# An attention and GLU kernel on one core: a planner's order replaced by an order written down as a string

## The chip, the cores and the metric

The kernel runs on one core of one Trainium2 chip. The metric is device time in microseconds, from one launch. The number of a kernel is the median of its runs; a profile is one further execution, with its own time.

## The reference

All arrays are float32, and all products must keep about that precision. The input x has 2048 tokens of 512 features.

```python
xn = layernorm(x)                                    # 2048 x 512
q, k, v = split(xn @ wqkv)                           # 32 heads of 16
p = softmax(q @ k.T * 16 ** -0.5)                    # per head, 2048 x 2048, no mask
s = (p @ v) @ wo                                     # heads joined
h = (xn @ w_gate) * (xn @ w_up)                      # 2048 x 1792
g = silu(h @ w_down)
out = x + s * g
```

## The kernel before

**Units and turns.** The 32 heads form eight groups of four, and the tokens four blocks of 512 queries. One group with one block is a unit; there are 32 units (`NU`). A unit takes 16 turns, one for each 128 keys. A turn needs, for each of the four heads, a transposed score (`expo`, called t): one matmul of 50 rows into a PSUM bank, and one exponential on ScalarE into an SBUF tile `e`. Then `pv` multiplies the four tiles with the values, for four heads side by side in the array's columns, and adds into one PSUM bank of its own. The trace shows a turn of `pv` as eight matmuls, and two turns in a row as sixteen.

**The maxima.** The exponentials need each query's row maximum, which is an extra operand row of the t matmul. So every score is also computed the other way round (`score`, called s), one matmul of 48 rows into a bank and one `tensor_reduce` on VectorE (the tile `mx`). When a unit has its 64 scores of this kind, `maxima` reduces them further on VectorE, with a small subtraction on GpSimd (`mm`), and `rest` transposes them (`mt`), stores them to DRAM (`MD`) and loads them into the rows of the query tile (`qs`). Only then may the unit's first t run. Scores run `LEAD` = 21 turns ahead of exponentials.

**Products.** Everything else on TensorE is a list of 202 outs, each a product of 128 x 512: projections of q and k (26), the GLU's gate and up products (112), its down products (48, in three thirds per token block), and the last projection (16). Float32 operands are split into a high and a low part on GpSimd, ScalarE and VectorE, and three terms are summed. An out uses the array by halves: all its terms for the lower 64 rows (code `f`), then, after a tiny read of the bank by ScalarE (`look`), all for the upper 64 rows (`F`). Scores t and s also use one half each, the lower (t, s) or the upper (T, S), by the head. Two matmuls on different halves run side by side, so TensorE's time is counted in slots of one lower and one upper matmul.

**Evacuation.** A finished projection or gate product, and the first third of a down product, is copied by ScalarE; an up product is multiplied with the gate by VectorE, then split (`hidden`); further thirds are added by VectorE. After a unit's last turn `heads` transposes the sums (VectorE), divides by the sum (`rc`, `on`), transposes back and stores (`OD`).

**Banks.** PSUM holds eight banks: one for `pv`, seven (`POOL`) for scores and outs.

**Order.** TensorE, ScalarE and VectorE run in the order in which the program issues their instructions; that of the other engines and of the DMA queue is left to the framework. The stretch `early` (layer norm, first projections, values, the first 84 scores) is laid out by hand and is not touched. Behind it, the class `Order` plans while the program is built: it keeps an estimated clock for each of the three engines, and in each `step` chooses what runs next, from constants at the head of the file (`SLOT`, `TURN`, `EXP_STEP`, `MAX_STEP` and the like). A slot with t on one half and s on the other goes first, then t or s with a product on the other half, then products; a `turn` of one or two batches of `pv` when their exponentials are thought to be done. It takes the bank that has been free longest. Evacuations and looks are queued as tasks with due times and run when the engine is thought idle. The last projection of the last token block lacks the last four heads (`kept`, `final`): these are added at the end by twelve more matmuls, when `last_heads` has split them; the loop at the end of `body` calls `final` for two tiles at a time as soon as they are ready.

```python
            if ops is None:
                ops = {x: "f" for x in (0, 1) if can[x]}
                if len(ops) < 2 and ready:
                    return self.turn(ks)
                if not ops:
                    return self.wake()
```

Of the kernel before, what the change touches and what calls it, by code (L numbers as in the profile page):

```python
# [19 lines left out]
P = 128  # L20
# [15 lines left out]
PACE, PACE0 = 4.95, 0  # L36
MOST = 4
HELD, T_APART, S_APART, APART = 2, 3, 6, .4
NEARLY, LEAN, AHEAD = 1, .1, 16
SLOT, ENTER, TURN, LEAVE, AGAIN = .229, .105, .857, .10, .105  # L40
T_SEEN, EXP_STEP, EXP_FREE, E_READY = .43, .494, .66, .65
S_SEEN, MAX_STEP, MAX_FREE = .46, .609, .75
COPY, HIDDEN, PRODUCT, LOOK, LOOK_SEEN, RECIP = .60, .63, .68, .16, .15, .30
MAXIMA, MAXIMA_WAIT, REST, KNOWN = .45, 4.0, .15, 6.0
RELEASE, IDLE, LATE, SPLIT_WAIT, SILU_GAP = .15, .1, 3.0, 12.0, 12.0
ACT_AHEAD, DVE_AHEAD, ACT_FULL, DVE_FULL = .5, .9, .75, 1.2
# [7 lines left out]
def body(ctx, tc, x, wqkv, wo, wg, wu, wd, out):  # L54
# [209 lines left out]
    class Out:  # L264

        def __init__(self, name, sums, evac, begin=None, ready=None, need=None, more=(), kept=False):
            self.name, self.sums, self.evac, self.begin = name, sums, evac, begin
            self.ready, self.need, self.more, self.kept = ready, need, more, kept
            self.looked = None
            self.over = False  # L270

        def open(self, k, o):
            self.bank, self.o = k, o
            if self.begin:
                self.begin()
            sums = self.sums()
            self.terms = [*(self.more() if self.more else ()), *sums], sums
            self.at = [0, 0]

        def blocked(self, x):  # L280
            return self.need is not None and not self.need(self.at[x], x)

        def product(self, x):
            n, ts = self.at[x], self.terms[x]
            rows = (LOWER, UPPER)[x]
            l, r = ts[n]
            last = n == len(ts) - 1
            nc.tensor.matmul(self.o, l[rows], r[rows], start=x == 0 and n == 0,  # L288
                             stop=last and (x == 0 or not self.kept), skip_group_check=x == 1)
            self.at[x] += 1  # L290
            return last

    class Order:

        def __init__(self, outs):
            self.pe = self.act = self.dve = 0.0
            self.free = [0.0] * POOL
            self.outs, self.next = outs, None
            self.low = self.high = None
            self.mid = []  # L300
            self.held = 0
            self.done = [0, 0]
            self.tpos, self.spos = [0, 0], [2 * LEAD, 2 * LEAD]
            self.tout, self.sout = [], []
            self.es, self.eready = {}, {}
            self.turns = self.begun = 0
            self.after = False
            self.tasks = {"act": [], "dve": []}
            self.number = 0
            self.known = {0: -100.0}  # L310
            self.fetch()

        def fetch(self):
            self.next = next(self.outs, None)

        def task(self, engine, ready, cost, fn, gate=None, urgent=False, then=None):
            self.number += 1
            self.tasks[engine].append((ready, self.number, cost, fn, gate, urgent, then))
            self.tasks[engine].sort(key=lambda t: t[:2])

        def run_tasks(self):
            again = True
            while again:
                again = False
                for engine in ("act", "dve"):
                    for n, (ready, _, cost, fn, gate, urgent, then) in enumerate(self.tasks[engine]):
                        if ready > self.pe:
                            break
                        idle = getattr(self, engine) <= self.pe + IDLE
                        if (idle or urgent or self.pe - ready > LATE) and (gate is None or gate()):  # L330
                            del self.tasks[engine][n]
                            begin = max(getattr(self, engine), ready)
                            setattr(self, engine, begin + cost)
                            fn()
                            if then:
                                then(begin + cost)
                            again = True
                            break

        def bank(self):  # L340
            k = min((t, k) for k, t in enumerate(self.free) if t is not None and t <= self.pe)[1]
            return k, pool(k)

        def banks(self):
            return sum(t is not None and t <= self.pe for t in self.free)

        def may_open(self):
            return (self.low is None and self.next is not None
                    and (self.held < HELD or self.held == HELD and self.nearly())
                    and (self.next.ready is None or self.next.ready()))  # L350

        def nearly(self):
            o = self.high
            return not self.mid[1:] and (o is None or len(o.terms[1]) - o.at[1] <= NEARLY)

        def lean(self, x):
            return LEAN * (AHEAD - (self.done[0] - self.done[1])) * (1 if x == 0 else -1)

        def can_low(self):
            if self.low is None:  # L360
                return self.may_open() and self.banks() > 0
            return not self.low.blocked(0)

        def can_high(self):
            if self.high is None:
                return bool(self.mid) and self.mid[0].looked is not None and self.mid[0].looked <= self.pe
            return not self.high.blocked(1)

        def do_low(self):
            if self.low is None:  # L370
                o, self.low = self.next, self.next
                k, bank = self.bank()
                self.free[k] = None
                self.held += not o.kept
                o.open(k, bank)
                self.fetch()
            o = self.low
            self.done[0] += 1
            if o.product(0):
                self.low = None  # L380
                self.mid.append(o)

                def done(t, o=o):
                    o.looked = t + LOOK_SEEN
                self.task("act", self.pe + T_SEEN, LOOK, lambda: nc.scalar.activation(look, o.o[0:1, 0:1], AF.Copy),  # L385
                          urgent=True, then=done)

        def do_high(self):
# [3 lines left out]
            self.done[1] += 1  # L392
            if o.product(1):
                self.high = None
                o.over = True
                if not o.kept:
                    def gone(t, o=o):
                        self.free[o.bank] = t + RELEASE
                        self.held -= 1
                    o.evac(self.pe + T_SEEN, gone)  # L400

        def do_t(self, x, late):
# [5 lines left out]
            k, o = self.bank()  # L408
            self.tpos[x] += 1
            i, kt = divmod(n, 16)  # L410
            e = expo(i, kt, j, o)
            begin = max(self.act, self.pe + T_SEEN + late)
            self.act = begin + EXP_STEP
            self.free[k] = begin + EXP_FREE
            self.tout.append(self.free[k])
            self.es.setdefault(n, {})[j] = e
            self.eready[n] = begin + E_READY

        def do_s(self, x, late):
            p = self.spos[x]  # L420
            r, j = p // 2, 2 * (p % 2) + x
            k, o = self.bank()
            self.spos[x] += 1
            si, sr = divmod(r, 16)
            score(si, sr, j, o)
            begin = max(self.dve, self.pe + S_SEEN + late)
            self.dve = begin + MAX_STEP
            self.free[k] = begin + MAX_FREE
            self.sout.append(self.free[k])
            if min(self.spos) == 32 * (si + 1) and max(self.spos) >= 32 * (si + 1) and sr == 15:  # L430
                self.task("dve", self.dve, MAXIMA, lambda: maxima(si), urgent=True,
                          then=lambda t: self.task("dve", t + MAXIMA_WAIT, REST, lambda: rest(si),
                                                   then=lambda t: self.known.__setitem__(si, t + KNOWN)))

        def turn(self, ks):
            for n in ks:
                pv(n // 16, n % 16, self.es.pop(n))
                del self.eready[n]
            self.turns += len(ks)
            self.pe += ENTER + TURN * len(ks) + LEAVE  # L440
            self.after = True
            if self.turns % 16 == 0:
                heads(self, self.turns // 16 - 1)

        def t_allowed(self, x):
            n = self.tpos[x] // 2
# [720 lines left out]
```

## Time and profile before

| | before |
|---|---|
| median of 3 runs | 1828.31 us (1823.27 to 1832.83) |
| profiled execution: time, span | 1832.05 us, 1830.3 us |
| TensorE busy | 1797.4 us, 13,568 matmuls |
| VectorE busy | 1433.9 us |
| ScalarE busy | 1238.7 us |
| GpSimd busy | 588.8 us |
| mean granted TensorE clock | 0.988 of full speed |
| first t matmul | 115.25 us after the span's start |
| start of the last batch of `pv` | 1808.37 us |

The span is that of the instructions on the core; the time also holds what lies around it. In the profile PE is TensorE, PEld its weight loads, DVE VectorE, ACT ScalarE, POOL GpSimd, SP the engine that issues the DMAs. A line of a group reads: line of the program, engine, operation, output<-inputs by the program's names, shapes, count | busy us, mean ns of one | idle time of its engine before them and what ended it. A line of the timeline has start us, length us and the group; `x8` is the number of instructions merged into it. In the chain of work that ended last a line has start us, length us and what held the end. A row of waits has the total in us, how often, and the longest. A row of stretches has the stretch, its length, the busy time of PE, PEld, DVE, ACT and POOL (instructions in brackets), the granted clock, and share and rate of the DMA engines.

### The profile page before, as it was taken

Reading aid. Unit: us, or ns where it says so; the run is one execution under the profiler, and the core shown is the slowest. Engines: PE = TensorE matmul, PEld = TensorE weight load, DVE = VectorE, ACT = ScalarE, POOL = GpSimd, SP = SyncE. Lnnn points to the kernel's source line nnn. Section 1 sums busy time; section 2 is a strip of 40 time slices with the busy share of each in tenths; the row PEclk is TensorE's granted clock in tenths of the full one; section 3 lists DMA queues with packets and bytes.
Section 4 is the critical chain, followed back from the end, with each engine's and each line's share of the span. In section 5 each row is a group of like instructions: output and inputs, shape, how many; then the busy total and the mean of one; then the engine's idle time right before and its main releaser. Section 6 shows DMA issues by size and latency. Waiting matters only on the chain.

```text
span 1830.3 us, 34996 instructions
## 1 busy us (share of the span) xinstructions
PE 1797.4 (98%) x13568; PEld 1057.7 (58%) x13568; DVE 1433.9 (78%) x2433; ACT 1238.7 (68%) x2487; POOL 588.8 (32%) x649
## 2 busy tenths in 40 slices
PE   8899999999999999999999999999999999999998
PEld 6566655565655565555555555656555665554555
DVE  7487877888878888878888788888887888878832
ACT  5147777776766767667676767767676777767674
POOL 5312333530523244143042523314163241332230
PEclk9899999999999999999999999999999999999999
DMA  5425532610231222321024211321234120112232
GB/s 196 112 67 188 200 127 103 159 52 22 73 74 50 77 67 68 62 64 51 22 81 108 80 39 57 70 43 53 73 91 91 33 68 25 56 39 85 71 121 70
DMA packets 117234, 145.79 MB, mean 80 GB/s; under 512 B 12620, under 2 KB 74060, under 8 KB 114380
## 3 DMA queue, kind: packets, MB, share of 16 engines
q1 hardware_dynamic: 117068, 143.55, 27.3%
q8 instruction: 107, 1.75, 0.4%
q14 instruction: 59, 0.48, 0.1%
HBM read 95.94 MB, written 47.45 MB: 78 GB/s over the span
## 4 chain that ended last, share of the span: by engine, by line
PE 92%; DMA 3%; DVE 2%; POOL 1%; ACT 1%; issue 0%; SPq 0%; ACTq 0%; POOLq 0%; DVEq 0%
PE b L288 32%; PE pv L980 26%; PE b L969 16%; PE b L941 15%; PE v L211 2%; DVE mx L943 1%; DMA qs<-MD 1%; PE p L211 1%; PE s L941 1%; DMA MD<-mt 0%; DMA ks<-KD 0%; ACT e L971 0%; DMA wdr<-in_wd_dram 0%; DMA qs<-QD 0%; DMA ks<-in_x_dram 0%
## 5 line engine op out<-in xcount | busy, mean ns | idle before, releaser
L943 DVE TENSOR_REDUCE mx<-b 128x1 f32<-128x512 f32 x1964 | 1232.8, 683 | 287.7 <-PE b L941 136.9
L971 ACT ACTIVATE e<-b 128x512 f32<-128x512 f32 x2048 | 1109.4, 600 | 475.4 <-PE b L969 242.2
L969 PE MATMUL b<-qs,ks 50*128 50x512 f32 x2048 | 776.3, 418 | 7.6 <-DMA qs<-MD 6.0
L941 PE MATMUL b<-ks,qs 48*128 48x512 f32 x1964 | 758.5, 424 | 0.7 <-DVE mx L943 0.3
L980 PE MATMUL pv<-e,V 128*32 128x512 f32 x4096 | 515.2, 605 | 0.2 <-DVE tr L1007 0.2
L969 PEld LDWEIGHTS b<-qs,ks 50*128 50x128 f32 x2048 | 366.4, 186 | 173.0 <-DVE mx L943 47.3
L941 PEld LDWEIGHTS b<-ks,qs 48*128 48x128 f32 x1964 | 338.8, 186 | 197.2 <-ACT e L971 66.4
L980 PEld LDWEIGHTS pv<-e,V 128*32 128x32 f32 x4096 | 98.8, 109 | 218.0 <-issue 207.7
L288 PE MATMUL b<-fh,w1h 64*128 64x512 f32 x504 | 201.0, 402 | 0.6 <-ACT look L385 0.3
L288 PE MATMUL b<-fh,w0h 64*128 64x512 f32 x500 | 199.1, 400 | 0.0
L288 PE MATMUL b<-fh,w1l 64*128 64x512 f32 x504 | 198.4, 398 | 0.0
L288 PE MATMUL b<-fl,w1h 64*128 64x512 f32 x504 | 197.8, 396 | 0.0
L288 PE MATMUL b<-fh,w0l 64*128 64x512 f32 x500 | 196.7, 397 | 0.0
L288 PE MATMUL b<-fl,w0h 64*128 64x512 f32 x500 | 196.6, 395 | 0.0
L288 PE MATMUL b<-dh,hh 64*128 64x512 f32 x448 | 162.7, 403 | 0.7 <-ACT hh L253 0.5
L288 PE MATMUL b<-dh,hl 64*128 64x512 f32 x448 | 158.9, 400 | 2.3 <-POOL hl L254 2.1
L288 PE MATMUL b<-dl,hh 64*128 64x512 f32 x448 | 158.6, 400 | 0.0
L288 PEld LDWEIGHTS b<-fh,w0h 64*128 64x128 f32 x500 | 92.8, 186 | 16.0 <-issue 5.7
L288 PEld LDWEIGHTS b<-fh,w1h 64*128 64x128 f32 x504 | 93.1, 186 | 15.5 <-issue 4.4
L288 PEld LDWEIGHTS b<-fh,w1l 64*128 64x128 f32 x504 | 93.2, 186 | 12.5 <-issue 6.7
L288 PEld LDWEIGHTS b<-fh,w0l 64*128 64x128 f32 x500 | 92.9, 186 | 9.2 <-issue 3.4
L288 PEld LDWEIGHTS b<-fl,w0h 64*128 64x128 f32 x500 | 92.9, 186 | 9.0 <-issue 2.9
(165 smaller groups left out, 1905.8 us busy)
## 6 DMA issues: line engine op xcount, KB each, us to landing
w1r<-in_wg_dram SPq DMA_DIRECT2D x56, 256.0 KB
w0r<-in_wu_dram SPq DMA_DIRECT2D x56, 256.0 KB
wdr<-in_wd_dram SPq DMA_DIRECT2D x56, 256.0 KB
qs<-QD SPq DMA_DIRECT2D x64, 192.0 KB
ks<-KD SPq DMA_DIRECT2D x12, 768.0 KB
KD<-hl SPq DMA_DIRECT2D x16, 512.0 KB
QD<-hl SPq DMA_DIRECT2D x16, 512.0 KB
OD<-tr SPq DMA_DIRECT2D x31, 256.0 KB
```

The lines of the kernel that those rows point to most:

```text
L211: nc.tensor.matmul(o, l(d), r(d), start=k == d == 0, stop=k == 2 and d == ND - 1)
L288: nc.tensor.matmul(self.o, l[rows], r[rows], start=x == 0 and n == 0, stop=last and (x == 0 or not self.kept), skip_group_check=x == 1)
L941: nc.tensor.matmul(o, QS[i][b:b + KB, pr, t * P:(t + 1) * P], k[b:b + KB, pr, kc * 512:(kc + 1) * 512], start=True, stop=True)
L943: nc.vector.tensor_reduce(MX[i][:, j, t, kc:kc + 1], o, axis=AX.X, op=OP.max)
L969: nc.tensor.matmul(o, k[b:b + KR, pr, kt * P:(kt + 1) * P], QS[i][b:b + KR, pr], start=True, stop=True)
L971: nc.scalar.activation(e, o, AF.Exp, scale=DH ** -0.5)
L980: nc.tensor.matmul(fst["pv"][32 * j:32 * j + 32], V[:, kt, h0:h0 + 32], es[j], start=kt == 0, stop=kt == NT - 1)
```

## The change

The planner goes. In its place stands a string, `ORDER`, of some 14,200 characters that a search over orders has found, and a class that reads it. Each letter issues one thing: t, T, s, S a score on the lower or upper half, with a digit for its PSUM bank; o (with a bank) the first lower matmul of the next out, f a further one, F an upper one; v and w one or two turns of `pv`; l a look; e and d an evacuation on ScalarE or VectorE; h the split of a hidden tile; y a quarter of the silu; m and r `maxima` and `rest`; x, c, b the three steps of `heads`; Q the load and split of one token block's heads for the last projection.

```diff
-PACE, PACE0 = 4.95, 0
...
-SLOT, ENTER, TURN, LEAVE, AGAIN = .229, .105, .857, .10, .105
...
+ORDER = """
+o0T1ffT2fS3fT4fT1ffS5fS6ffs3S2fS4o1ls5fS6fFfFfFfFfFfFfFfFfFfFs3Fls2Fs4S5eo6FfFfFt3Ft0FfFt2FfFs4Fs3Ft5S0fFfFfS2efT4fS5f
...
+fFfFfFfFfFfFo3FlfFfdfFfFfFfFfFfFfFfFfFvlxFFFcFbFFFFF
+"""
...
+        def t(self, x, k):
             p = self.tpos[x]
             n, j = p // 2, 2 * (p % 2) + x
             if n == self.begun:
                 self.begun += 1
                 round_begins(n)
             self.tpos[x] += 1
+            self.es.setdefault(n, {})[j] = expo(*divmod(n, 16), j, pool(k))
...
+            if min(self.spos) == 32 * (i + 1):
+                def whole():
+                    maxima(i)
+                    self.then("r", lambda: rest(i))
+                self.then("m", whole)
...
+        def run(self, order):
+            codes = iter(order)
+            for code in codes:
+                if code in "ts":
+                    getattr(self, code)(0, int(next(codes)))
+                elif code in "TS":
+                    getattr(self, code.lower())(1, int(next(codes)))
+                elif code == "o":
+                    self.low_product(int(next(codes)))
+                elif code == "f":
+                    self.low_product()
+                elif code == "F":
+                    self.high_product()
+                elif code in "vw":
+                    for _ in range("_vw".index(code)):
+                        self.v()
+                elif code == "Q":
+                    prepare(int(next(codes)))
+                else:
+                    self.todo[code].pop(0)()
...
         order_ = Order(outs(wq0))
-        todo = list(range(4))
-        while not order_.over():
-            order_.step()
...
+        order_.run(ORDER.replace("\n", ""))
+        last_heads()
+        for t in range(4):
             final(t)
```

The functions that evacuate an out (`evac` and its tasks with due times) become plain functions that the letters e, d, h and y call, and `ending_outs` loses its conditions of readiness. `last_heads` and all four `final` now stand behind the whole string.

656 lines of the change are left out of this document (273 added, 383 removed).

## Prediction

> **What bounds the kernel now.** I read the page first: busy time by engine, the shares of the chain that ended last, and the costliest groups.
>
> ```profile
> span 1830.3 us, 34996 instructions
> ...
> PE 1797.4 (98%) x13568; PEld 1057.7 (58%) x13568; DVE 1433.9 (78%) x2433; ACT 1238.7 (68%) x2487; POOL 588.8 (32%) x649
> ...
> PE 92%; DMA 3%; DVE 2%; POOL 1%; ACT 1%; issue 0%; SPq 0%; ACTq 0%; POOLq 0%; DVEq 0%
> ...
> L943 DVE TENSOR_REDUCE mx<-b 128x1 f32<-128x512 f32 x1964 | 1232.8, 683 | 287.7 <-PE b L941 136.9
> L971 ACT ACTIVATE e<-b 128x512 f32<-128x512 f32 x2048 | 1109.4, 600 | 475.4 <-PE b L969 242.2
> L969 PE MATMUL b<-qs,ks 50*128 50x512 f32 x2048 | 776.3, 418 | 7.6 <-DMA qs<-MD 6.0
> L941 PE MATMUL b<-ks,qs 48*128 48x512 f32 x1964 | 758.5, 424 | 0.7 <-DVE mx L943 0.3
> L980 PE MATMUL pv<-e,V 128*32 128x512 f32 x4096 | 515.2, 605 | 0.2 <-DVE tr L1007 0.2
> ```
>
> TensorE is the bound: it is 98% busy and carries 92% of the chain, while VectorE and ScalarE wait for it. But a busy PE hides its losses here, because a matmul is shown for 0.39 us and the next pair starts 0.23 us later. So the second view is the timeline of PE, read by starts.
>
> ```profile
> 115.25 0.49 PE L969 MATMUL b<-qs,ks 50*128 50x512 f32 x1
> ...
> 119.54 1.06 PE L980 MATMUL pv<-e,V 128*32 128x512 f32 x8
> ...
> 601.07 0.39 PE L941 MATMUL b<-ks,qs 48*128 48x512 f32 x1
> ...
> 605.54 0.40 PE L288 MATMUL b<-fh,w1l 64*128 64x512 f32 x1
> ...
> 605.91 1.92 PE L980 MATMUL pv<-e,V 128*32 128x512 f32 x16
> 607.76 0.49 PE L941 MATMUL b<-ks,qs 48*128 48x512 f32 x1
> ...
> 608.10 0.39 PE L969 MATMUL b<-qs,ks 50*128 50x512 f32 x1
> ...
> 644.11 0.39 PE L288 MATMUL b<-dh,hh 64*128 64x512 f32 x1
> 644.43 1.06 PE L980 MATMUL pv<-e,V 128*32 128x512 f32 x8
> 645.42 0.50 PE L288 MATMUL b<-dl,hh 64*128 64x512 f32 x1
> ...
> 1808.37 1.93 PE L980 MATMUL pv<-e,V 128*32 128x512 f32 x16
> ```
>
> The work is made of slots and batches. In a slot one matmul on the lower 64 rows and one on the upper 64 run side by side; a slot with one half empty costs the same. From 601.07 to 605.54 there are 19 steps: 0.235 us a slot (median of all undisturbed steps 0.234). A batch is one turn of four-head products (x8) or two (x16). From its start to the next slot a double takes 607.76 - 605.91 = 1.85 and a single 645.42 - 644.43 = 0.99 (medians 1.854 and 0.996), so a turn is 0.858 and 0.138 is fixed. The last slot before a batch is 0.32 to 0.37 long (median 0.331, 0.097 over a slot), the first behind it 608.10 - 607.76 = 0.34 (0.104 over). A batch thus costs 0.138 + 0.097 + 0.104 = 0.339 us besides its turns.
>
> Up to the last batch at 1808.37 I counted, by the order of the trace and the row half that the program gives each matmul, 4,604 slots and 340 batches with 510 turns (the first at 119.54). That makes 4604 x 0.234 + 340 x 0.339 + 510 x 0.858 = 1077.3 + 115.3 + 437.6 = 1630.2 us. It took 1808.37 - 115.25 = 1693.1. So 62.9 us are waits, and what follows in the slow clock behind them. The third views, waits, chain and stretches, say where:
>
> ```profile
> PE b L969 <- DMA qs<-MD: 6.0, 4, 2.3
> ...
> PE b L288 <- POOL hl L254: 2.1, 2, 1.7
> ...
> PE b L288 <- ACT look L385: 0.3, 1, 0.3
> ```
> ```profile
> 528.63 2.03 DVE mx L943 x4
> ...
> 531.86 1.94 DMA MD<-mt
> ...
> 534.11 6.78 DMA qs<-MD
> ...
> 541.02 0.46 PE b L969
> ```
> ```profile
> 541.80:545.20 3.40, 3.40 (x17) 3.01 (x16) 1.93 (x3) 2.70 (x7) 0.00 (x0) 0.50 0.99 136
> 545.20:548.60 3.40, 3.40 (x30) 2.77 (x27) 2.99 (x6) 3.27 (x7) 0.00 (x0) 1.00 0.23 31
> ...
> 1650.00:1705.00 55.00, 54.02 (x320) 24.30 (x322) 46.62 (x80) 38.88 (x77) 16.16 (x19) 0.91 0.24 73
> 1705.00:1760.00 55.00, 54.56 (x390) 30.13 (x386) 40.26 (x70) 36.34 (x72) 14.65 (x15) 0.97 0.30 95
> ```
>
> Comparing each stretch between two batches with these prices: 12.0 us lie at four places where the row of maxima of the next unit (mt, MD, qs) comes late, as at 541.02; there the granted clock then falls to 0.50 for 3.4 us (17 matmuls in the time of 30). 21.6 us lie behind 1618 us, 11.4 of them from 1650 to 1705. The other 29.3 us are spread, some 7 ns a slot.
>
> **The change part by part.** It adds and removes no work on PE, ScalarE or VectorE that I can find: the string's letters count the same 2,048 t, 1,964 s, 2,520 lower and 2,508 upper products, 512 turns and 202 looks (l). Loads, splits and stores are called from the same places, so SP and POOL get the same list. What changes is order.
>
> *Slots.* Reading the string with the same pairing rule gives 4,546 slots before the last batch, against 4,604; 4,526 would be perfect. 58 x 0.234 = 13.6 us less on PE's path, which nothing else covers.
>
> *Batches.* The string has 193 doubles (w) and 126 singles (v), 319 in all, for 171 and 170. Before the last one that is 318 batches with 511 turns: 318 x 0.339 + 511 x 0.858 = 107.8 + 438.4 = 546.2 for 552.9, 6.7 us less. Slots and batches: 1610.0 for 1630.2, 20.2 us less.
>
> *The tail.* Before, 39 slots of products and two groups of finals (L891) come behind the last batch. Now there are nine upper products, and all twelve finals.
>
> ```profile
> 1810.38 0.72 DVE L1007 STREAM_TRANSPOSE tr<-pv 128x512 f32<-128x512 f32 x1 [2.15 <-PE pv L980]
> ...
> 1813.31 0.50 PE L891 MATMUL b<-hl,g 128*128 128x512 f32 x1 [0.98 <-ACT look L385]
> ...
> 1814.58 0.69 DVE L786 TENSOR_TENSOR y<-b,y 128x512 f32<-128x512 f32 x1 [0.60 <-PE b L891]
> ...
> 1825.81 0.69 DVE L783 TENSOR_TENSOR y<-b,hh 128x512 f32<-128x512 f32 x1
> ```
>
> Now: from the single batch to the transpose 2.01 - 0.86 = 1.15 (1810.38 - 1808.37, one turn less); from there to the first final 1813.31 - 1810.38 = 2.93, which covers the nine products (9 x 0.234 = 2.1); to the first end on VectorE 1.27; then six VectorE operations of 0.69 (one for even, two for odd tiles) = 4.14, longer than the finals that feed them; then 3.8 as now from the last of them (1826.50) to the span's end, 1830.3. Sum 13.3 us for 1830.3 - 1808.37 = 21.9: 8.6 less. If the finals ran at half clock it would be some 2 us worse.
>
> *The waits.* What the string can't order is when DMAs land. By the same prices it keeps 5.6 us or more between r and the first t of the next unit (before: 5.4 or more), so I leave the 12.0 as they are; bounds 0 and, at four more places, 24. From 1650 to 1705 the old order runs out of filler: 44 product matmuls in the sixteen turns of unit 29, against 123 in the string. There VectorE's maxima, 0.62 each back to back,
>
> ```profile
> 1662.27 2.48 DVE L943 TENSOR_REDUCE mx<-b 128x1 f32<-128x512 f32 x4 [0.34 <-PE b L941]
> ```
>
> need 62 x 0.62 = 38.4, some 41.5 with VectorE's other work there, where PE's slots and batches need 40.3; in the string it is 60 x 0.62 = 37.2, some 42.4 in all, and PE needs 45.6. So the 11.4 goes. VectorE is next, at 0.93 of PE in that unit. By the stretch 1650 to 1705 at clock 0.91, 5.0 of these 11.4 us is slow clock. By the Trainium skill ("TensorE: Matmul & The Clock Gate", the part on the clock gate) the gate closes after an idle window of about 3.4 us, and no wait here is so long; then those 5.0 us would have another cause and stay, and the sum would end 5.0 higher. The rows above disagree: the wait at 541.02 was 2.3 us at most, and the halved stretch follows at once.
>
> Spread waits: a bank used again within four slots of its last score is what PE waits for most. The old order has 79 such uses, the first and last at
>
> ```profile
> 242.37 0.50 PE L941 MATMUL b<-ks,qs 48*128 48x512 f32 x1
> ...
> 1807.01 0.50 PE L969 MATMUL b<-qs,ks 50*128 50x512 f32 x1
> ```
>
> and they hold 10.9 us, 4.6 of it before 1618 us. The string has 18 of them: 3.5 less. The last hidden row of a third (hl) now comes 2.6 us or more before its first use, for 0.0 to 0.2 in the old order at the ends of the token blocks; that was the wait of 2.1. Against this, the upper half of a product follows the last lower matmul after three slots in 14 places, for one, with ScalarE's look between: 0.3 each by the one row that shows it, 4.2 at most, of which I take a third. So 3.5 + 2.1 - 1.4, some 4 us, come off the spread 29.3; bounds: 5 more, and 15 off. So waits are 12.0 + 10.2 + 25.3 = 47.5 for 62.9, 15.4 less.
>
> **Sum.** 20.2 + 8.6 + 15.4 = 44.2 us less: a span of 1786.1 for 1830.3. The profiled execution took 1832.05, 3.7 above the median of the runs, 1828.31; against the median I forecast 1784. Runs of before differ by 0.5%, so 0.5% is about what a measurement can tell from no change.
>
> **Rivals.**
> 1. The waits don't shrink, since order moves a wait rather than ends it: VectorE at 0.93 in the late unit is near its limit. Only slots, batches and tail are left: 1828.3 - 28.8 = 1799.5. For it: 29.3 us of waits have no single cause. Against: distances grew.
> 2. The maxima come late more often. Of the 31 units the string gives 13 less than 6.3 us between m and r, where only three had that little before. Each miss costs 3 us (12.0 / 4), so eight more give 1808.
> 3. Slower: seven PSUM banks turned over at fixed distances make PE wait shortly but so often that the clock falls again and again. Each half-clock stretch loses 1.7 us (3.4 at 0.50). From 1784 it takes 32 more of them to pass 1837.5 (0.5% slower); 35 give 1844. Against it: the old order turns over the same seven banks, and
>
> ```profile
> 200.00:500.00 300.00, 299.83 (x2396) 178.33 (x2394) 242.79 (x409) 216.18 (x440) 105.19 (x116) 1.00 0.33 99
> ```
>
> shows the clock at 1.00 over 300 us of it. The Trainium skill describes this failure (same page, "A second HAM failure mode: psum-queue depth-cycling"); no run here shows it so far.
> 4. The order doesn't do what it says, because POOL and SP aren't in the string and their queues set the pace: no change, 1828. Against: POOL is busy 32%, and PE waited for it 2.1 us in the products.
>
> **How the numbers follow.** Forecast (waits of 30 to 60 us, 1768 to 1797) 0.70; rival 1 0.12; rival 2 0.06; rival 4 or a mixture within 0.5% 0.05; rival 3 0.03; waits below 30, 0.04. Faster 0.92, same 0.05, slower 0.03. From 1768 up to 1806 the range holds the forecast's own range, rival 1 and half of rival 2, some 0.84.
>
> **What would show it.** 319 batches; 0.234 a slot and 0.339 a batch unchanged; no stretch below clock 0.95 from 1600 us to the last batch; 13 us from the last batch to the end; a stretch from the first t to the last batch of some 1657. If the clock row shows many slices under 9, or mx waits on mt, rivals 3 or 2 hold. The forecast is wrong most simply if unlisted waits grow: half a slot per batch more would be 37 us.

## The result, and the profile after

The changed kernel takes 1780.03 us (median of 4 runs, 1774.98 to 1784.14), the old one beside it 1828.99 us (4 runs): a ratio of 0.9734, 95% interval 0.9692 to 0.9775. The prediction was 1784 (1768 to 1806). Of the four runs after, two took 1775.0 and 1776.4 us at a mean granted clock of 0.996, and two 1783.6 and 1784.1 us at 0.992 and 0.991. The profiled execution after took 1776.43 us, 3.6 below its median, while that of before lay 3.1 above; so the two traces differ by 55.6 us where the medians differ by 49.

The page of the changed kernel: span, busy time, granted clock in 40 slices, shares of the chain that ended last, and the costliest groups.

```profile
span 1774.6 us, 34733 instructions
...
PE 1746.1 (98%) x13568; PEld 1050.1 (59%) x13568; DVE 1424.7 (80%) x2433; ACT 1232.7 (69%) x2487; POOL 587.9 (33%) x649
...
PEclk9999999999999999999999999999999999999999
...
PE 92%; DVE 2%; DMA 2%; POOL 2%; issue 1%; ACT 0%; SPq 0%; POOLq 0%; ACTq 0%; DVEq 0%
...
L839 DVE TENSOR_REDUCE mx<-b 128x1 f32<-128x512 f32 x1964 | 1218.5, 683 | 249.2 <-PE b L837 161.8
L867 ACT ACTIVATE e<-b 128x512 f32<-128x512 f32 x2048 | 1096.6, 601 | 395.4 <-PE b L865 230.2
L865 PE MATMUL b<-qs,ks 50*128 50x512 f32 x2048 | 724.8, 416 | 6.0 <-DMA qs<-MD 4.7
```

The counts are those of before (13,568 matmuls, 1,964 maxima, 2,048 exponentials) and so is the mean length of one. PE is as busy as it was, 98%, and carries the same 92% of the chain. Nothing on this page but the span, PE's shorter busy time and the smaller idle columns tells that the kernel became faster, and nothing tells why: a bound engine shows its gain only when its starts are counted.

The timeline of the end, as it was read before:

```profile
1761.42 1.06 PE L876 MATMUL pv<-e,V 128*32 128x512 f32 x8
...
1762.56 0.72 DVE L903 STREAM_TRANSPOSE tr<-pv 128x512 f32<-128x512 f32 x1 [1.81 <-PE pv L876]
...
1765.48 0.50 PE L787 MATMUL b<-hl,g 128*128 128x512 f32 x1 [0.72 <-ACT g L794]
...
1766.74 0.69 DVE L708 TENSOR_TENSOR y<-b,y 128x512 f32<-128x512 f32 x1 [0.59 <-PE b L787]
```

The last batch starts at 1761.42 and the span ends 13.2 us later. The first t starts at 113.99 (115.25 before).

The stretches from 1600 us to the last batch (length; busy PE, PEld, DVE, ACT, POOL; granted clock; DMA), and what PE waits for:

```profile
1600.00:1660.00 60.00, 59.41 (x470) 34.10 (x470) 53.42 (x90) 42.35 (x86) 21.57 (x24) 1.00 0.24 76
1660.00:1710.00 50.00, 49.68 (x391) 28.15 (x391) 39.06 (x67) 36.90 (x77) 22.63 (x24) 1.00 0.39 124
1710.00:1759.00 49.00, 49.00 (x382) 28.71 (x379) 9.06 (x14) 34.27 (x75) 9.57 (x10) 1.00 0.28 97
```
```profile
PE b L865 <- DMA qs<-MD: 4.7, 3, 1.9
...
PE b L865 <- DVE mx L839: 1.3, 1, 1.3
...
PE b L396 <- POOL hl L366: 0.6, 1, 0.6
```

The clock is 1.00 in all three, where it was 0.91 and 0.97. From 1600 to 1710 VectorE works 92.5 of 110 us; before, from 1650 to 1760, it worked 86.9.

The ledger goes by starts of matmuls and row halves. Its slots are counted as the experiments below showed to be right: between two batches the lower and the upper matmuls are counted apart, and the larger number is what is paid ("by balance"). The prices, measured again after, are the same: 0.234 a slot, 1.854 a double, 0.996 a single. The batches are counted in the trace: 315 of them, where the prediction counted 319 letters. At four places two letters stand side by side (vv or vw), and the trace has one batch there; the three vv take 1.854 us, as a double does.

| | before | after | less |
|---|---|---|---|
| first t, from the span's start | 115.25 | 113.99 | 1.3 |
| slots before the last batch x 0.234 | 4597: 1075.7 | 4544: 1063.3 | 12.4 |
| batches: count x 0.339 + turns x 0.858 | 340, 510: 552.9 | 314, 511: 544.9 | 8.0 |
| waits and slow clock (the rest) | 64.5 | 39.2 | 25.3 |
| last batch to the span's end | 21.9 | 13.2 | 8.7 |
| span | 1830.3 | 1774.6 | 55.7 |

In the tail, 30 slots fewer lie behind the last batch (9 for 39: 7.0 us) and the batch is a single (0.86); what is left, 0.8, is the tail itself. The first t comes between 113.0 and 117.7 us in the runs below that leave the early stretch as it is, so the 1.3 in the first row can't be told from no change.

### The profile page after: what moved, and what is told of

Its sections match the earlier page's. It is cut to its first block, busy times and chain, and to the rows that moved or that the text cites. A ratio compares the mean times of both kernels' runs of the same rounds, so it can differ in the third digit from the quotient of the medians.

```text
span 1774.6 us, 34733 instructions
## 1 busy us (share of the span) xinstructions
PE 1746.1 (98%) x13568; PEld 1050.1 (59%) x13568; DVE 1424.7 (80%) x2433; ACT 1232.7 (69%) x2487; POOL 587.9 (33%) x649
## 4 chain that ended last, share of the span: by engine, by line
PE 92%; DVE 2%; DMA 2%; POOL 2%; issue 1%; ACT 0%; SPq 0%; POOLq 0%; ACTq 0%; DVEq 0%
PE b L396 33%; PE pv L876 26%; PE b L865 15%; PE b L837 14%; PE v L323 2%; DVE mx L839 1%; PE s L837 1%; DVE st L262 1%; DMA qs<-MD 1%; DMA ks<-KD 0%; POOL dl L564 0%; PE p L323 0%; DMA wdr<-in_wd_dram 0%; POOL xl L298 0%; DMA hh<-in_x_dram 0%
## 5 line engine op out<-in xcount | busy, mean ns | idle before, releaser
L839 DVE TENSOR_REDUCE mx<-b 128x1 f32<-128x512 f32 x1964 | 1218.5, 683 | 249.2 <-PE b L837 161.8
L867 ACT ACTIVATE e<-b 128x512 f32<-128x512 f32 x2048 | 1096.6, 601 | 395.4 <-PE b L865 230.2
L865 PE MATMUL b<-qs,ks 50*128 50x512 f32 x2048 | 724.8, 416 | 6.0 <-DMA qs<-MD 4.7
L837 PE MATMUL b<-ks,qs 48*128 48x512 f32 x1964 | 683.9, 415 | 0.0
L876 PE MATMUL pv<-e,V 128*32 128x512 f32 x4096 | 504.8, 600 | 0.0
L865 PEld LDWEIGHTS b<-qs,ks 50*128 50x128 f32 x2048 | 344.5, 185 | 169.2 <-ACT e L867 72.5
L837 PEld LDWEIGHTS b<-ks,qs 48*128 48x128 f32 x1964 | 330.2, 185 | 175.2 <-DVE mx L839 83.0
L237 POOL CAST w0h<-w0r 128x512 fp32r<-128x512 f32 x60 | 36.6, 611 | 226.2 <-PE b L396 207.3
L396 PEld LDWEIGHTS b<-fh,w1l 64*128 64x128 f32 x504 | 92.9, 186 | 15.1 <-issue 10.9
L396 PEld LDWEIGHTS b<-fh,w0l 64*128 64x128 f32 x500 | 92.5, 186 | 13.9 <-issue 9.2
```

The source lines that it names most:

```text
L237: cast = nc.gpsimd.tensor_copy(hi, raw)
L837: nc.tensor.matmul(o, QS[i][b:b + KB, pr, t * P:(t + 1) * P], k[b:b + KB, pr, kc * 512:(kc + 1) * 512], start=True, stop=True)
L839: nc.vector.tensor_reduce(MX[i][:, j, t, kc:kc + 1], o, axis=AX.X, op=OP.max)
L865: nc.tensor.matmul(o, k[b:b + KR, pr, kt * P:(kt + 1) * P], QS[i][b:b + KR, pr], start=True, stop=True)
L867: nc.scalar.activation(e, o, AF.Exp, scale=DH ** -0.5)
L876: nc.tensor.matmul(fst["pv"][32 * j:32 * j + 32], V[:, kt, h0:h0 + 32], es[j], start=kt == 0, stop=kt == NT - 1)
```

## Experiments: is it the order, and what are the banks worth?

The theory after the result: nothing but the order and the bank digits made the gain, in three parts (slots, batches, waits), and the waits shrank more than predicted because of the banks. Rivals: reading a string removes something else (the class that plans, the loop at the end); or the banks don't matter, since the order alone moves the waits.

**old_order.** The planner's own order of before, written down as a string and read by the new class.

```diff
 ORDER = """
-o0T1ffT2fS3fT4fT1ffS5fS6ffs3S2fS4o1ls5f...
+t0S1o2S3fT4ffS5fT6fs0T1t4S3ffT6fT5fS1ft0fS4v...
```

> The planner's own order, with its banks, written as a string and read by the new class; only the finals of the first two tiles move from the middle of the tail to its end. Theory (the change is the order and nothing else): as before, about 1828, less 1 to 2 us for the tail; waits before the last batch again near 63 us. Rival (the way in which the new class issues loads and tasks brings part of the gain): 1800 or less.

1825.14 us, ratio 0.9984 (0.9972 to 0.9995). The waits are 59.4 us, the tail 20.2. So the way the order is issued is worth some 3 us (0.9 to 5.1 by the interval), of which the tail is 1.7, and the change is the order and its digits. Against this kernel the waits of the new order are 20.1 less. Split by unit, 13.0 of them lie in units 28 to 30 (17.3 to 4.3; unit 29, the one of 1650 to 1705, 10.3 to 1.6) and 7.1 in all others. That its waits are 5 us under the 64.5 of before, with the same order, is slow clock: the trace of before has three halved stretches of 3.4 us (at 1627, 1695 and 1740) that this one hasn't.

**banks_planner.** The new order, with the digits given out by a rule like the planner's: the bank that is thought to have been free longest, by estimated times of the engines. 72 uses lie within four slots of the bank's last score with no batch between, for 18 in the string.

```diff
-o0T1ffT2fS3fT4fT1ffS5fS6ffs3S2...
+o0T1ffT2fS3fT4fT5ffS6fS1ffs2S3...
```

> The new order of instructions with the banks dealt by the planner's rule (the bank whose estimated release is earliest): 72 uses within four slots, for 18, nearly all of the new ones at four slots. Theory (uses at two and three slots cost 0.4 to 0.9 us, at four some 0.2): 10 to 25 us more than the new order, 1790 to 1805, so that the digits of the banks are a part of the gain of their own. Rival (any sensible rule does as well, the order is all): within 5 us.

1797.63 us, ratio 0.983 (0.9807 to 0.9852): 17.6 more than with the string's digits. Waits are 61.0, no less than in the old order, though unit 29 has only 4.2. So the order empties the late stretch, and the digits take away the rest: when only digits are changed, 21.7 us of waits come back in the traces. By the medians it is 17.6; 3.4 of the 21.7 are two more halved stretches of the clock in this execution.

**banks_oldest.** The new order; each score takes the bank whose last use lies longest back.

```diff
-...T4fT1ffS5fS6ffs3S2fS4o1ls...
+...T4fT5ffS6fS1ffs2S3fS4o5ls...
```

> The new order with the banks dealt out by another rule, always the free bank that has been idle longest, products' first matmuls included: 143 uses of a bank within four slots of its last score, for 18. Theory (0.14 us for each such use, 10.9 us over 79 in the old order): 125 x 0.14, some 17 us more, about 1797. Rival (the digits of the banks do nothing, since the engines that empty them set the pace): within 5 us of the new order.

1885.73 us, ratio 1.0321 (1.03 to 1.0342): 105.7 more than the string's digits, and six times what was expected. The estimate priced a near use at 0.14 us, as the prediction had it (79 uses, 10.9 us). What a use costs depends steeply on its distance: at two slots 0.7 to 1.0 us, at three 0.4 to 0.6, at four 0.16 to 0.28. By the steps between slots, some 50 of the 146.0 us of waits lie at such uses and some 60 at uses at five to seven slots. Three rows (one of each kernel) of the stretch from 1000 to 1500 us: the string's digits, the planner's rule, the oldest bank.

```profile
1000.00:1500.00 500.00, 500.00 (x4012) 295.18 (x4006) 422.64 (x716) 368.54 (x746) 164.95 (x180) 1.00 0.23 61
```
```profile
1000.00:1500.00 500.00, 499.80 (x3981) 295.66 (x3979) 420.02 (x712) 367.90 (x741) 171.49 (x187) 1.00 0.24 64
```
```profile
1000.00:1500.00 500.00, 489.63 (x3707) 277.97 (x3705) 397.20 (x665) 346.13 (x691) 156.80 (x171) 1.00 0.24 62
```

The instructions in brackets are what to read: 4,012 matmul records against 3,707 in the same time, 8% fewer, while PE still counts as busy for 98% of it. And the clock is 1.00 in all three. This is rival 3 of the prediction with its first half true (banks that come round too soon do make PE wait, some 100 us of it) and its second half false: PE's longest idle time there is 1.1 us, and between the first t and the last batch no stretch is at half clock. What the Trainium skill describes ("TensorE: Matmul & The Clock Gate", "A second HAM failure mode: psum-queue depth-cycling"), a clock that falls again and again from such pauses, did not show here, at a mean granted clock of 0.995 over the whole run.

**banks_even.** A try at a better version: each use takes the bank that would be free longest by the changed kernel's own rows, with a floor on the distance in slots, so that only 6 uses lie within four slots, and 355 within five for 769.

```diff
-...T4fT1ffS5fS6ffs3S2fS4o1ls...
+...T4fT5ffS6fS1ffs2S3fS4o6ls...
```

> The new order with other bank digits: each score and product takes the bank that this kernel's rows of timing would leave free longest, with a floor on the distance in slots, so that 6 banks are used again within four slots (18 with the string's own digits) and 355 within five (769). Theory (the price of a bank is its distance in slots): 12 uses fewer at 0.2 to 0.4 us, 3 us less, and up to 2 more from the fifth slot: 1775 to 1780 us, waits of PE 32 to 37 us. Rival (the string's own digits are already at the floor, what waits are left being late rows of maxima): 1780, no difference that can be told. Rival (what counts is when the engines let go of a bank, which a distance in slots doesn't say): more waits at other places, 1785 or more.

1839.28 us, ratio 1.0058 (1.0039 to 1.0078): 59 more than the string's digits and 0.6% slower than the kernel before. The theory fell, far beyond the second rival's 1785. Counting by who reads the bank shows what was given up:

| bank last read by (a single batch counted as five slots, a double as nine) | uses | at 5 slots | at 6 | at 7 |
|---|---|---|---|---|
| VectorE (s), string's digits | 1964 | 57 | 315 | 284 |
| VectorE (s), even digits | 1964 | 54 | 543 | 376 |
| ScalarE (t), string's digits | 2047 | 694 | 334 | 157 |
| ScalarE (t), even digits | 2047 | 295 | 438 | 329 |

The string takes the freshest banks from ScalarE and leaves VectorE's alone longer; evening out the distances moved 320 uses of VectorE's banks to six and seven slots. There the price differs at the same distance: where a t or s takes an s bank again at six slots, its step is 47 ns longer than a slot with the even digits (25 us in 539 uses) and 14 ns with the string's (303 uses). So a distance in slots is not the price. What fits both is whether the reader has got through its queue by then, and the traces show it. Take the k-th t with the k-th exponential and the k-th s with the k-th maximum: in none of the thirteen traces of kernels with a string does a t or s start less than 0.052 us after the instruction that read its bank last has ended. One that starts within 0.07 us of that end is counted here as held up by its reader. Of some 3,800 uses such a start is found in 141 with the string's digits, 230 with the planner's rule, 354 with the even digits and 461 with the oldest bank, and the waits go the same way: 39.2, 61.0, 104.7 and 146.0 us. At six and seven slots, VectorE's banks have 14 such starts in 585 uses with the string's digits and 214 in 912 with the even ones. The waits of PE, as the profile lists them for this kernel:

```profile
PE b L865 <- DMA qs<-MD: 4.9, 3, 2.5
PE b L837 <- DVE mx L839: 2.5, 8, 0.6
...
PE b L865 <- ACT e L867: 1.0, 2, 0.8
PE b L396 <- DVE mx L839: 1.0, 3, 0.6
PE b L865 <- DVE mx L839: 0.9, 3, 0.5
```

The four rows that name the banks' readers show 5.4 us of 65 (waits by the ledger: 104.7 for 39.2). A delay that only spaces the starts of overlapping matmuls is not in this list.

## Experiments: what is a slot?

The prediction paired matmuls in the order of the program: each lower one with the next upper one if that stands beside it, a slot for each that finds none. The rival: a half doesn't wait for the other half's turn, so only the balance between two batches counts.

**unpaired.** 204 places of four products where the halves alternate now have two lower ones first, then two upper ones. By the prediction's rule that is 121 slots more.

```diff
-4o1ls5fS6fFfFfFfFfFfF...
+4o1ls5fS6ffFFffFFffFF...
```

> The new order with two lower matmuls and then two upper ones at the 204 places where a pair of slots held only products (ffFF for fFfF): by the pairing rule 121 more slots. Theory (a half-empty slot costs a whole one, 0.234 us): 28 us more than the new order, about 1808. Rival (TensorE is not bound by pairing, since waits follow anyway): under 8 us more.

1779.83 us, ratio 0.9743 (0.9719 to 0.9767): the time of the new order. The rule was wrong. The timeline of PE for four products which stand in the program as lower, lower, upper, upper:

```profile
900.49 0.39 PE L396 MATMUL b<-fh,w0h 64*128 64x512 f32 x1
900.60 0.39 PE L396 MATMUL b<-fh,w1l 64*128 64x512 f32 x1
900.72 0.39 PE L396 MATMUL b<-fl,w0h 64*128 64x512 f32 x1
900.83 0.39 PE L396 MATMUL b<-fh,w1h 64*128 64x512 f32 x1
```

w0 are the weights of an up product, whose lower half runs here, w1 those of the gate product before it, whose upper half does. The upper matmul of 900.60 stands third in the program and starts second: it overtakes a lower one that still waits for its half. (The profile has starts, not TensorE's queue; that the queue is in the program's order is how the kernel is built.) The Trainium skill ("TensorE: Matmul & The Clock Gate", in the part on packing small matmuls, "The mechanism") says that matmuls start and end strictly in program order; in this trace, across the two row halves, they start in another.

**runs_apart.** How far does it reach? In 182 runs of 2 to 11 slots of products all lower ones come first, then all upper ones.

```diff
-4o1ls5fS6fFfFfFfFfFfFfFfFfFfFs3F...
+4o1ls5fS6ffffffffffFFFFFFFFFFs3F...
```

> The new order with every run of product slots (fFfF..., 182 runs of 2 to 11 slots) written as all lower matmuls and then all upper ones. Theory now (a matmul may start before one ahead of it that waits for the other half, so only the balance of halves between two batches counts, however far the two lie apart): as the new order, within 5 us of 1780. Rival (the overtaking reaches over one or two instructions only): the 19 runs of 3 or more lose some 70 slots, 16 us, and the time is about 1796.

1784.4 us, ratio 0.9758 (0.9736 to 0.978), 4.4 more, waits 44.6 for 39.2. The time is the theory's, but "however far the two lie apart" doesn't hold: 162 of the 182 runs have two slots only, and the long ones do lose. The timeline of a run of seven (lower matmuls with w1 and w0, upper ones with hl and dh):

```profile
1762.56 0.40 PE L396 MATMUL b<-fh,w1l 64*128 64x512 f32 x1
1762.80 0.40 PE L396 MATMUL b<-fh,w1h 64*128 64x512 f32 x1
1763.04 0.39 PE L396 MATMUL b<-fl,w1h 64*128 64x512 f32 x1
1763.27 0.39 PE L396 MATMUL b<-fh,w1l 64*128 64x512 f32 x1
1763.28 0.50 PE L396 MATMUL b<-fh,hl 64*128 64x512 f32 x1
```

Three lower matmuls start alone, 0.23 us apart; the first upper one starts beside the fourth and so passes three that still wait. In the run of eleven that starts at 1757.69 it starts beside the eighth (1759.31) and again passes three. Runs of three and four cost nothing; the six runs of seven to eleven that show a loss took 0.35 to 1.3 us longer than the same matmuls in the new order, 4.6 us together, which is nearly all of the loss.

**early_lower.** 52 lower products, out of stretches with as many upper ones, stand ahead of a batch instead of behind it. By balance that is 52 slots more.

```diff
-...fFfT3fFwecfS6o0S2l...
+...fFfT3fFfwecS6o0S2l...
```

> The new order with 52 lower product matmuls moved from behind a batch to just before it, so that nothing is finished later: counted by the larger half of each stretch, 52 more slots, uses of a bank within four slots as in the new order (21 for 18). Theory (balance of halves between batches, 0.234 us for each slot, and the rest of the unbalanced kernel's loss was products finished late): 12 us more than the new order, about 1792, waits unchanged near 38. Rival (a half-empty slot costs some 0.65 us, as the unbalanced kernel's stretches show): 34 us more, about 1814.

1789.94 us, ratio 0.9789 (0.977 to 0.9808). From the first t to the last batch it takes 1659.74 us for 1647.43: 12.3 more, and 52 x 0.234 = 12.2 (9.9 more by the medians of the runs). The waits are 39.4, as before the edit (39.2). This is the slot's price by itself.

**unbalanced.** The same with 102 upper products, moved to just behind a batch.

```diff
-...FfT3fFt5FfS2fS0fT3wels...
+...FfT3ft5FfS2fS0fT3wFels...
```

> The new order with 102 upper products moved from before a batch to just behind it, so that the stretch before has one lower too many and the one behind one upper too many: counted as the larger half of each stretch, 102 more slots, with the same matmuls. Theory (balance between batches is what a slot costs, 0.234 each): 24 us more than the new order, about 1804; uses of a bank within four slots rise from 18 to 60, which may add some 6. Rival (pairing does not matter at all, as the unpaired order seemed to say): within 6 us.

1849.07 us, ratio 1.0112 (1.0089 to 1.0135): 69 more, where 24 to 30 were expected. The 102 stretches that got an upper product are 0.68 us longer on average, not 0.234. From the first t to the last batch it takes 76.5 us more, of which 102 x 0.234 = 23.9 are slots. The rest, 52.6 us, is waits and slow clock: a product whose last upper matmul comes behind a batch ends later, so its bank and its tile do too. The list of waits shows a part of it.

```profile
PE b L396 <- ACT look L423: 6.5, 11, 0.8
PE b L837 <- DVE h L604: 5.4, 12, 0.7
```

The moved matmul's own cost can't be read from this run; early_lower, which moves starts and not ends, gives it.

## Experiments: batches

**split_doubles.** 112 doubles become two singles, the second a place later: 112 batches more (427 in the trace for 315).

```diff
-...fS5ffT3wls0T1t4Fs2...
+...fS5ffT3vls0T1vt4Fs2...
```

> The new order with 112 of its 193 double batches split into two singles with one slot between: 431 batches for 319, the slots the same. Theory (0.339 us of TensorE's time for each batch, covered by nothing): 112 x 0.339 = 38 us more than the new order, about 1818. Rival (the fixed part of a batch is time in which ScalarE and VectorE catch up, so that it comes off the waits elsewhere): less than 15 us more.

1816.35 us, ratio 0.9943 (0.992 to 0.9967): 36.3 more. First t to last batch, 1684.1 - 1647.4 = 36.7, by 112 is 0.327 us a batch, against the prediction's 0.339. The waits are 37.9 for 39.2, so little else changed.

**merged.** The other way: 28 batches move up to stand right behind the one before.

```diff
-...FfT1s6FfFwes4T0t1T5vrt0...
+...FfT1s6FfFwves4T0t1T5rt0...
```

> The new order with 28 batches moved up to stand directly behind the one before, where their exponentials were due by then: 291 uninterrupted stretches of turns for 319. Theory of the batch alone: 28 x 0.339 = 9.5 us less, about 1771. Against it stand 130 uses of a bank within four slots for 18, at 0.1 to 0.2 us each 11 to 22 us more. I expect the second to win: 1780 to 1795; a time under 1775 would say that the search stopped short.

1798.05 us, ratio 0.9833 (0.9812 to 0.9853): 18 more. The trace has 288 batches for 315: 27 x 0.339 = 9.2 is saved, and 27.5 is lost in waits (66.7 for 39.2). Scores that stood between two batches now crowd behind them, and 130 uses of a bank lie within four slots. The digits were left as they are, so this says that the string's digits allow no fewer batches at these places; whether other digits would isn't shown.

## Experiments: the late rows of maxima

The prediction left 12.0 us at the places where a unit's row of maxima (mt, MD, qs) comes late. In the changed kernel the chain ahead of one such row goes through a load of weights that stands before it on SP and waits for a buffer:

```profile
780.83 2.64 DMA wdr<-in_wd_dram
...
783.53 0.62 POOL dh L563
...
784.22 1.29 POOL dl L564
...
786.27 2.24 DMA qs<-MD
...
788.64 0.47 PE b L865
```

Two theories: the row's DMAs are queued on SP behind loads that wait for a buffer (dl); or the loads are in their way wherever they are issued.

**rows_by_pool.** GpSimd issues the row's store and loads.

```diff
-        dma(MD[i].rearrange("f (b q) -> b f q", b=4), mt)
+        nc.gpsimd.dma_start(MD[i].rearrange("f (b q) -> b f q", b=4), mt)
```

> The new order with the three DMAs that carry a unit's row of maxima (MD, qs) issued by GpSimd, not from the one queue on SyncE where they stand behind other loads. Theory (late rows, some 10 us in the new order's profile, come from standing behind loads that wait for GpSimd's splits): 5 to 10 us less, 1770 to 1775. Rival (the rows come late because the DMA engines are busy, or GpSimd's own list delays them as much): within 4 us, or slower where the splits wait.

1808.65 us, ratio 0.9893 (0.9873 to 0.9914): 28.6 more. The gain that the theory promised isn't there. The waits and the chain of this run:

```profile
PE b L865 <- DMA qs<-MD: 25.0, 9, 13.8
```
```profile
947.16 7.67 DMA MD<-mt
...
955.68 11.77 DMA qs<-MD
```

At this place the store took 7.67 us and the load 11.77 from issue to landing, where the chain above has 2.24 for such a load. That is not the price of GpSimd's issuing: the median of these loads in this run is 2.1 us. Here the DMA engines were full (share 0.98 and 0.85 in the two stretches), with loads of 1 MB (fl, fh) and 768 KB (ks) that SP had issued between 945.77 and 950.7:

```profile
947.00:955.00 8.00, 6.83 (x53) 3.82 (x49) 7.58 (x13) 1.09 (x3) 3.23 (x3) 1.00 0.98 322
955.00:968.00 13.00, 0.42 (x2) 0.45 (x4) 0.13 (x1) 0.00 (x0) 1.11 (x2) 0.59 0.85 135
```

So at this one row the rival is right, the DMA engines are busy. For the others the run doesn't decide.

**loads_by_pool.** The rows stay on SP; GpSimd issues the loads of the weights.

```diff
-        dma(raw, src.rearrange("(d p) f -> p d f", p=P))
+        nc.gpsimd.dma_start(raw, src.rearrange("(d p) f -> p d f", p=P))
...
-            dma(raw, wd[f * P:(f + 1) * P])
+            nc.gpsimd.dma_start(raw, wd[f * P:(f + 1) * P])
```

> The new order with the weight loads (w0r, w1r, wdr) issued by GpSimd, whose splits they wait for, so that SyncE's queue holds no load that waits for GpSimd and the rows of maxima pass at once. Theory (rows come late by standing behind such loads): the late rows of units 3, 12 and 16 go, 5 to 10 us less than the new order, 1770 to 1775. Rival 1 (the rows are late because the DMA engines are busy with the loads themselves): within 4 us. Rival 2 (issuing costs GpSimd time, and splits come late): slower.

1801.83 us, ratio 0.9858 (0.9833 to 0.9883). The first t comes 15.7 us later (129.7), a cost of the early stretch, and waits are 49.4. Of the late rows of units 3, 12 and 16 the first two went (0.9 us of waits left in each unit), that of unit 16 stayed (3.8), and units 10 and 17 got late ones (5.0 and 4.9).

```profile
PE v L323 <- POOL e L963: 9.5, 4, 8.2
PE b L865 <- DMA qs<-MD: 5.1, 3, 2.0
```

Rival 2, that splits come late, is in it too: the wait of 8.2 us lies in the early stretch. So it isn't SP's queue alone. What makes a given row late stays open but for the one above.

## Why the prediction was right, and where it wasn't

**The bound** held: the same prices for slot, double and single, PE at 92% of the chain.

**Slots**: 13.6 us predicted, 12.4 by balance. The size came out and the reason didn't, so the size was luck. The step "by the order of the trace and the row half", a slot for each neighbour missing, is refuted by unpaired; the count by balance between batches is confirmed by early_lower. The two rules agree here because both orders keep their halves nearly alternating.

**Batches**: 6.7 predicted, 8.0 in the ledger. The step that was off is "319 in all": the prediction counted letters, and the trace has 315 batches. The price held, 0.327 by split_doubles for 0.339.

**Tail**: 13.3 predicted, 13.2 measured.

**Waits**: by the prediction's count of slots 62.9 to 47.5; with the trace's 315 batches they fell to 38.8. This is the term that was mis-sized, by 8.7 us in these two traces. By the medians the miss is less: a gain of 44.2 was forecast and 49.0 measured, for 55.7 between the two profiled spans. The term had three parts. The late stretch went as forecast: unit 29 has 1.6 us left of 11.7, and the clock there is 1.00. The spread waits were the miss. The prediction counted uses of a bank within four slots, priced each at 0.14 us and took 3.5 us off; banks_planner shows that the digits are worth 21.7 us of waits (17.6 by the medians), and the other runs show two things that made its price too low: a near use costs 0.16 to 1.0 us by its distance (banks_oldest), and uses at five to seven slots, which the count left out, cost too where the reader's queue is long (banks_even). How the 21.7 divide between the two isn't settled, but for the 3.4 of slow clock. The row of maxima was left at 12.0; units 0, 3, 12 and 16 hold 13.0 us (2.3, 3.0, 4.4, 3.3) where the median unit has 0.9, so some 9 us lie there and that part was about right to leave. The predicted stretch from first t to last batch, 1657, came to 1647.4: 10 us, the same miss and the batches.

**The slow clock**: the 5.0 us that hung on it went. The old trace has halved stretches at seven places behind 115 us (3.4 us each, one of 6.8), the new one at two; in both the last lies behind the last batch. The other of the new trace comes behind the late row at 788.64:

```profile
788.60:792.00 3.40, 3.35 (x21) 2.90 (x23) 1.81 (x3) 2.17 (x5) 1.29 (x1) 0.76 0.45 142
792.00:795.40 3.40, 3.40 (x23) 1.75 (x22) 2.71 (x5) 1.82 (x4) 1.89 (x2) 0.74 0.52 133
```

Two windows at about 0.75 are one halved stretch, from 790.39 to 793.80, that lies across both. An earlier row of the same trace kept PE waiting longer and was not followed by one:

```profile
327.14 0.46 PE L865 MATMUL b<-qs,ks 50*128 50x512 f32 x1 [1.93 <-DMA qs<-MD]
...
788.64 0.47 PE L865 MATMUL b<-qs,ks 50*128 50x512 f32 x1 [1.65 <-DMA qs<-MD]
```

The starts of the halved stretches tell why. Within a trace they lie on a grid: those of before at 541.80, 1401.95, 1627.23, 1668.19, 1695.50 and 1739.87 us are whole multiples of 3.413 us apart. On the grid of the new trace the idle 1.65 us (787.0 to 788.64) lies in one window, 786.98 to 790.39, and the 1.93 us (325.21 to 327.14) is cut at 326.18 into 0.97 and 0.96. In the fourteen traces of this case, from 116 us to the last batch and by the ends of matmuls that the profile gives, 28 windows have 1.5 us or more without a matmul, and half clock follows every one. Of those with less, only a few have it behind them: one with 1.36 us, windows that were at half clock themselves, and four in the late stretch of the old order (16 matmuls from 1664.78 to 1668.19, where 30 fit). So whether a late row costs 1.7 us more depends on where it falls on the grid. In unpaired's trace PE is idle for 1.88 us before 327.34, in banks_planner's for 1.88 before 330.58, the same row; half clock follows in the second only. The Trainium skill's page ("TensorE: Matmul & The Clock Gate", the part on the clock gate) asks for an idle window of about 3.4 us; that was again not reached before the clock halved.

**The rivals.** Rival 1 (waits don't shrink, 1799.5) has the time of the order with the planner's digits, 1797.63, but not by its mechanism, VectorE at its limit in the late unit: unit 29 has 4.2 us there for 10.3. The digits are what it left out. Rival 2 (more late rows): three waits of 4.7 us in sum for four of 6.0, and one of 1.3 (before 951.23) that the list puts down to mx. Rival 3 (the clock falls again and again): once between the first t and the last batch here, never in banks_oldest. Rival 4: old_order shows that the order with its digits is all of it but some 3 us.

## What to carry to other kernels

When an engine is busy 98% of the time, price its starts, not its busy time, and keep a ledger of slots, groups and a rest: here 25.3 of 55.7 us were in the rest, and of 65 us of waits in banks_even the list named 5.4. Two matmul streams on different row halves need the same number of matmuls between the points where both must stop, not strict alternation; in these traces one half could run three matmuls ahead. Which PSUM bank an instruction gets is a schedule of its own, here worth 17.6 of 49 us. None of the three rules tried (oldest, estimated release, free time with a floor on the distance) found digits as good as the string's, so measure: count the matmuls that start right behind the end of their bank's last reader.

## What the hardware showed that was not expected

- A matmul on one half of the rows goes past earlier ones of the other half, past three of them in the runs of seven and eleven (1763.28, 1759.31 us in runs_apart).
- The same seven banks under the same order span 1780 to 1886 us by digits alone, at a mean granted clock of 0.992 to 0.996 in the profiled executions.
- Half clock comes and goes on a grid of 3.41 us: 28 of 28 windows of that length with 1.5 us or more without a matmul were followed by it; a wait of 1.93 us cut by the grid was not, one of 1.65 within a window was.
- A load whose median from issue to landing is 2.1 us took 11.77 where the DMA engines were 0.85 to 0.98 busy with loads of 768 KB and 1 MB.
